# Attention and an S4 convolution on one core: two weight loads on another queue, and another order of the start

## The chip, the cores and the metric

One core of one Trainium2 chip. The metric is the device time of one launch in microseconds, the median of several runs. A core has TensorE (PE, matmuls), VectorE (DVE), ScalarE (ACT), GpSimd (POOL) and SyncE (SP, which here only issues DMAs), each with an instruction stream of its own; ACT and POOL issue DMAs too. The streams wait for each other on semaphores.

## The reference

```python
x = A_x                                   # 1 x 2048 x 448, bf16
g = sigmoid((x * gate_w).sum(-1))         # one gate per row
# a: attention, 16 heads of 28, one K and one V for all heads
q, k, v = x @ wq, x @ wk, x @ wv
a = softmax(q k^T / sqrt(28)) v, heads side by side, @ wo
# b: an S4 convolution of x along the rows, 448 channels, 256 modes
dt = exp(log_dt)
K[d, l] = Re sum_n C[d, n] * exp(dt * A[d, n] * l) * dt * B[d, n]
b = causal convolution of x with K, + x * Dskip    # the reference goes by FFT
out = g * a + (1 - g) * b
```

`A_re, A_im, B_re, B_im, C_re, C_im` are 448 x 256, and the output is 2048 x 448 in bf16. (In the setup the convolution's input is a tensor `u`, but the result uses `x` for both halves.)

## The kernel before, in words

**The attention.** The 2048 rows are four quarters of 512, the 16 heads four groups of 4: 16 blocks of one quarter and one group, each 64 tiles of 128 keys x 512 queries, 1024 tiles in all. `main` takes them in sets of 3 and 2 tiles. For each set PE makes the scores in PSUM (`qk`: line 1323 with four heads' rows of the array side by side from `qT`, or line 1332 as full matmuls from `qM`, a copy of `qT` by DMA with zeros for the other heads), ACT makes the exponential into `expT` (line 1357, 410 of them), and PE multiplies by V into `psB` (line 1383). Behind each block come the evacuation of `psB` and the division (`norm`, with a detour of the denominators through DRAM by POOL's DMAs), `outp` (multiplication by wo) and `fold` (gate and sum into `O`). `norm_last` does the division without the detour for the last two blocks.

**The convolution.** DVE builds tables of powers for 32 channels at a time (`masters`, `tables`, lines 991 to 1075); PE makes from them the taps K (`kgen`), which DVE puts into `kstg` and POOL's queue stores to `KP_scratch` in DRAM. SP loads them back as Toeplitz tiles T (`tload`, line 1131; 224 DMAs of 512 KB), PE multiplies them with `U`, a layout of x (`conv`, line 1155, two convs of 16 channels to each table), and DVE adds the result into `O`.

**The start.** `loads` issues the inputs. SP's queue carries, in this order: x's quarters 0 and 3 (natural layout, into `tab`), B_A_re and B_A_im as DMA transposes, wq, x's quarters 1 and 2 (`DQ`) as DMA transposes, and the other four parameters as DMA transposes. ACT's queue carries log_dt, wk, wv and the gate's weights. `prep_x` transposes quarters 0 and 3 on PE (line 718), evicts them to `xT` on ACT (line 728) where the pair (quarter, tile) is in `XA`, else on DVE (line 730), multiplies by wk (line 736), takes the largest |K| (line 742), and evicts K to `kT` on DVE (line 746) where the quarter is in `KD`, else on ACT (line 750). `Wb`, from the largest |K|, gives each query its offset below zero through one more matmul (`qproj`, line 963). `prep_params` computes the start values of the tables on DVE and ACT; ACT changes its function table three times (lines 862, 896, 911). The V weights are copied by DVE at line 645, the gate's at line 647.

**The order of everything.** No engine's order is written by hand. `Prog` collects all operations with their dependences and an estimated cost, and `schedule` puts them in order as a list planner: again and again it takes, of all ready operations, the one that can start first, ties by priority `pr` (lower first) and then by the place in the program. DMAs have an issue cost (`ISSUE`), a landing time (`DMA_NS` and `extra`) and a share of the DMA engines. Two things are special:

- Until the goal, the first exponential, operations that are not DMAs are picked by the length of the path from them to the goal, to which `RANK` adds a number of nanoseconds for single operations. `RANK` comes from a search. After the goal it has no effect.
- `idle` puts filler matmuls (line 1398, they add zero to `psB`) behind a PE operation where the planned matmul work of the last `SPAN` = 3413 ns is under `LOW` x `SPAN`, if the planned time is within `FILL` and the variable `part` is below 15:

```python
if self.part < 15 and self.FILL[0] < r < self.FILL[1] and busy < self.LOW * span:
...
pg.parts[len(pg.ops) - 1] = v % 16 if t < HF - 64 else 15
```

`HF` is 960, and `v` counts groups of four tiles.

Of the kernel before, what the change touches and what calls it, by code (L numbers as in the profile page):

```python
# [15 lines left out]
D = 448  # L16
H = 16
DH = 28
# [17 lines left out]
TW = 4 * 1024  # L36
XQ = NT * 512
SIN2PI = 6.2831850
XA = ((0, 1), (0, 2), (0, 3), (1, 0), (2, 2), (2, 3), (3, 0), (3, 1), (3, 2), (3, 3))
KD = (0, 1, 3)  # L40
GX = 3
DQ = (1, 2)
VNS = 140
# [32 lines left out]
def dram(t, off, dims):  # L76
    return bass.AP(tensor=t.tensor, offset=t.offset + off, ap=[list(d) for d in dims])
# [7 lines left out]
class Prog:  # L85
    SEM_NS = 56
    DMA_NS = 2200
    ISSUE = {"pool": 540.0, "sp": 470.0, "act": 470.0}
    LAT = {"pe": 170.0, "act": 173.0, "dve": 82.0, "pool": 85.0, "sp": 60.0}
    SAME = {"act": 100.0, "dve": 125.0, "pool": 150.0}  # L90
    SWITCH = 105.0
    BLOCK, FIRST, FETCH, IDLE, NEED = 256, 192, 5900.0, 3300.0, .015
    HALF = (21000.0, 21000.0, 1.8)
    HEAD = 0.6
    RANK = {111: 3000, 62: 3000, 39: -6000, 20: -3000, 30: -6000, 190: -6000, 46: -6000, 29: 700, 65: -6000, 84: 6000, 195: 6000, 40: -6000, 38: 3000, 33: 6000}
    POOL = (7,)
    LOW, SPAN, FILL = .53, 3413.0, (36000.0, 440000.0)
    AHEAD = 1500.0
    SLACK = {"pe": 700.0, "dve": 150.0}

    def __init__(self, nc, es):
        self.nc, self.es = nc, es
# [45 lines left out]
    def dma(self, pairs, desc, slot, rd=(), wr=(), pr=0, eng="sp", slow=False, extra=0, flip=False, cost=None, early=False):  # L148
        kw = dict(allow_slow_non_contiguous=True) if slow else {}

        def fn(e):
            if flip:
                return [e.dma_start_transpose(o, i) for o, i in pairs]
            return [e.dma_start(o, i, **kw) for o, i in pairs]  # L154
        nd, size = desc
        ns = 10.0 if size < 64 else 13.0 + 0.033 * size if size < 1500 else 8.0 + 0.0372 * size
        if cost is None:
            cost = nd * ns / 16.0 * (1.15 if size < 1500 else 1.0 if nd >= 512 else 1.4 if size < 3000 else 1.25)
        o = self.op(eng, fn, cost, rd, wr, pr)
        o.slot, o.ndma, o.extra = slot, len(pairs), extra + 200 * (early or flip)  # L160
        o.iss = len(pairs) * (1400.0 if flip else 640.0 if early else self.ISSUE[eng])
        prev = self.slots.get(slot)
        if prev is not None:
            o.deps[prev] = 1
        self.slots[slot] = o.i
        return o
# [268 lines left out]
def el(n, rate=0.96, fix=68):  # L435
    return fix + n / rate
# [22 lines left out]
class Kernel:  # L459
# [131 lines left out]
    def loads(self):  # L591
        pg, ins = self.pg, self.ins
# [33 lines left out]
        lx(QO[1])  # L626
        lraw(1)
        lraw(0)
        pg.dma(rows(wst, 0, ins["A_wq"], D), (448, 896), "wq", wr=["wqs"], cost=1500)
        lx(QO[2])  # L630
        lx(QO[3])
        pg.dma(rows(wks, 4 * DH, ins["A_wv"], DH), (448, 56), "wv", wr=["wvs"], eng="act", cost=150)
        pg.dma([(wks.v(0, P, 8 * DH, [[2, 3]]), dram(ins["gate_w"], 0, [[1, P], [P, 3]])),
                (wks.v(0, 64, 8 * DH + 6, [[1, 1]]), dram(ins["gate_w"], 384, [[1, 64], [1, 1]]))], (448, 2), "wg", wr=["wgs"], slow=True, eng="act", cost=150)
        for q in DQ:
            lx(q, True)
        pg.op("pool", lambda e: e.tensor_copy(self.Wk.v(0, P, 0, [[32, 16], [1, DH]]),
# [25 lines left out]
        for q in range(4):  # L663
            for j in (0, 2):
                u = 15 - 4 * q - j
                if q in DQ:
# [4 lines left out]
                    rd=[("xst", q)], wr=[("uf", q, j)], pr=0.6)  # L671
# [406 lines left out]
    def kgen(self, c):  # L1078
# [33 lines left out]
        for q in range(2):  # L1112
            lst = [(dram(self.KP, (32 * c + 16 * q + 4 * g) * KW, [[64, 32], [KW, 4], [1, 64]]),
                    ko.v(32 * g, 32, 256 * q, [[64, 4], [1, 64]])) for g in range(4)]
            pg.dma(lst, (512, 128), f"kw{q}", rd=["kst", "ksk"], wr=[("KP", c, q)], pr=0, eng="pool", extra=1800)

    def tbufs(self):
        n = NC * 8
# [19 lines left out]
    def conv(self, c):  # L1138
# [50 lines left out]
        pg.op("dve", lambda e: e.tensor_tensor(ov, ov, px.v(0, P, 0, [[1, 16], [16, 16]]), ALU.add),  # L1189
              el(256), rd=[Y], comm=tuple(("O" if c < 26 else "Oz", q) for q in range(7)), pr=2, unlock=px)  # L1190

    def outp(self, qc, tt):
        pg = self.pg
# [10 lines left out]
    def fold(self, qc, tt, px, off, n, rd, unlock=None):  # L1204
        tl = 4 * qc + tt
        ov = self.O.v(0, P, D * tl + off, [[1, n]])
        self.pg.op("dve", lambda e: e.scalar_tensor_tensor(ov, px(), self.gt.v(0, P, tl, [[1, 1]]), ov, ALU.mult, ALU.add),
                   el(n), rd=rd + ["gt"], comm=(("O", qc + tt * (qc == 3)), ("Oz", qc + tt * (qc == 3))), pr=2, unlock=unlock)

    def norm(self, i):  # L1210
        pg = self.pg
# [20 lines left out]
    def norm_last(self, i, o, n, bank, key):  # L1232
# [54 lines left out]
    def main(self):  # L1287
# [25 lines left out]
        def qk(s):  # L1313
# [165 lines left out]
```

## Time and profile before

| | |
|---|---|
| median of 3 runs | 506.75 us (506.19 to 508.49) |
| the profiled execution | 507.17 us, span 505.3 us, mean granted clock 0.985 |
| ACT busy | 482.6 us (96%), 466.2 of it in the 410 exponentials of line 1357 |
| DVE busy | 455.0 us (90%) |
| PE busy | 448.2 us (89%) |
| POOL busy | 165.3 us (33%) |
| first exponential | starts at 22.89 us |
| DMA | 139.51 MB, mean 276 GB/s |

Times in the profile are microseconds from the first instruction. A group's line gives busy time and mean duration (ns), then the engine's idle time before the group and what ended it. In a timeline a line gives start, duration, engine, source line, operation, output and inputs, and in brackets the idle time before it. In a table of windows each engine has its busy time and its number of instructions (x), then come the granted TensorE clock, the DMA engines' share and GB/s. "issue" is time in which an engine waited for nothing that the profile shows.

### The profile page before, as it was taken

How to read it: one execution, taken by the hardware profiler on the slowest of the kernel's cores; microseconds unless marked ns; L12 is line 12 of the kernel's file. 1: busy time of each engine (PE TensorE's matmuls, PEld its weight loads, DVE VectorE, ACT ScalarE, POOL GpSimd, SP SyncE). 2: the span in 40 equal slices, each digit the busy share in tenths (PEclk: the TensorE clock that was granted, in tenths of full speed). 3: DMA queues.
4: the chain of work that ended last, by engine and by line, in shares of the span. 5: the costliest groups of instructions: out<-in, count | busy, mean ns of one | idle time of the engine just before them, and what ended most of it. 6: DMA issues, size and time to landing. Idle time of an engine off the chain costs nothing.

```text
span 505.3 us, 18926 instructions
## 1 busy us (share of the span) xinstructions
PE 448.2 (89%) x8469; PEld 195.1 (39%) x8469; DVE 455.0 (90%) x834; ACT 482.6 (96%) x432; POOL 165.3 (33%) x308
## 2 busy tenths in 40 slices
PE   6797778898998999989898899999899999999885
PEld 2322213343433434334433344344343444344453
DVE  6899999999999999999999999999999999922334
ACT  5899999999999999999999999999999999999892
POOL 8533224252143520615332321435232152451000
PEclk8889999999999999999999999999999999999899
DMA  9977901979949797999989999599999979899982
GB/s 188 224 210 129 59 22 50 340 226 365 363 153 332 244 317 250 269 361 324 366 282 371 318 317 362 199 339 369 356 283 345 369 233 384 264 358 369 385 302 47
DMA packets 123395, 139.51 MB, mean 276 GB/s; under 512 B 56169, under 2 KB 63370, under 8 KB 123314
## 3 DMA queue, kind: packets, MB, share of 16 engines
q1 hardware_dynamic: 112208, 128.89, 79.8%
q0 software_dynamic: 8656, 9.25, 6.7%
q8 instruction: 66, 1.08, 0.9%
q10 hardware_dynamic: 2450, 0.17, 0.4%
q14 instruction: 15, 0.12, 0.1%
HBM read 125.18 MB, written 5.22 MB: 258 GB/s over the span
## 4 chain that ended last, share of the span: by engine, by line
ACT 48%; DVE 38%; PE 10%; issue 2%; DMA 1%; SPq 1%
ACT expT L1357 48%; DVE tab L1048 5%; DVE tab L1059 3%; DVE tab L1060 3%; DVE msq L991 3%; DVE tab L1070 2%; DVE tab L1058 2%; DVE tab L1057 2%; DVE mbf L1011 2%; PE psS L1332 2%; PE psB L1383 2%; DVE seedz L995 2%; PE psS L1323 2%; DVE seedz L993 1%; DVE tmp L1066 1%
## 5 line engine op out<-in xcount | busy, mean ns | idle before, releaser
L1357 ACT ACTIVATE expT<-psS 128x1536 bf16<-128x1536 f32 (+1 forms) x410 | 466.2, 1332 | 5.8 <-PE psS L1323 2.7
L1332 PE MATMUL psS<-qM,kT 128*128 128x512 bf16 (+2 forms) x455 | 122.5, 360 | 13.8 <-ACT expT L1357 10.5
L1383 PE MATMUL psB<-expT,vaug 128*32 128x512 bf16 (+2 forms) x1152 | 103.4, 366 | 3.1 <-issue 2.0
L1323 PE MATMUL psS<-qT,kT 29*128 29x512 bf16 (+2 forms) x699 | 82.1, 362 | 22.9 <-ACT expT L1357 21.5
L154 POOL DMA_DIRECT2D KP_scratch<-kstg x112 | 61.1, 553 | 65.6 <-DVE kstg L1110 37.4
L1048 DVE TENSOR_TENSOR tab<-tab,mbf 128x512 bf16<-128x512 bf16 (+3 forms) x56 | 64.6, 1154 | 0.0
L1383 PEld LDWEIGHTS psB<-expT,vaug 128*32 128x32 bf16 x1152 | 27.6, 93 | 76.1 <-issue 71.2
L154 POOL DMA_DIRECT2D rdenB<-R_scratch x56 | 28.4, 513 | 62.6 <-DMA R_scratch<-denT 53.7
L1332 PEld LDWEIGHTS psS<-qM,kT 128*128 128x128 bf16 x455 | 28.4, 97 | 50.7 <-ACT expT L1357 33.3
L1323 PEld LDWEIGHTS psS<-qT,kT 29*128 29x128 bf16 x699 | 21.4, 91 | 67.4 <-ACT expT L1357 53.6
L154 POOL DMA_DIRECT2D qM<-qT x64 | 32.2, 511 | 37.8 <-DVE qT L966 22.1
L1059 DVE TENSOR_TENSOR tab<-tab 128x1024 bf16<-128x1024 bf16 (+4 forms) x70 | 41.6, 595 | 0.0
L1060 DVE TENSOR_TENSOR tab<-tab 128x128 bf16<-128x128 bf16 (+4 forms) x70 | 41.5, 594 | 0.0
L1155 PE MATMUL psS<-T,U 128*32 128x128 bf16 (+3 forms) x1504 | 35.3, 220 | 0.3 <-DVE qT L966 0.3
L154 POOL DMA_DIRECT2D denT<-acc x14 | 10.0, 715 | 74.8 <-DVE kstg L1106 37.1
L1070 DVE TENSOR_TENSOR tab<-tab,tmp 128x4096 bf16<-128x4096 bf16 x14 | 32.0, 2285 | 0.1
L1058 DVE TENSOR_TENSOR tab<-tab,mbf 128x4096 bf16<-128x4096 bf16 x14 | 31.9, 2279 | 0.0
L1057 DVE TENSOR_TENSOR tab<-tab,mbf 128x4096 bf16<-128x4096 bf16 x14 | 31.9, 2276 | 0.0
L1155 PEld LDWEIGHTS psS<-T,U 128*32 128x32 bf16 (+3 forms) x1504 | 24.9, 94 | 13.8 <-issue 9.4
L1155 PE MATMUL psX<-T,U 128*32 128x128 bf16 (+7 forms) x1216 | 28.8, 222 | 0.1
L991 DVE TENSOR_TENSOR msq<-seedz 128x384 f32<-128x384 f32 (+1 forms) x50 | 27.1, 542 | 0.2
L1066 DVE TENSOR_TENSOR tmp<-tmp,mq 128x64 bf16<-128x64 bf16 (+4 forms) x70 | 25.3, 362 | 0.1
(160 smaller groups left out, 544.2 us busy)
## 6 DMA issues: line engine op xcount, KB each, us to landing
T<-KP_scratch SPq DMA_DIRECT2D x170, 512.0 KB, 9.1
U<-KP_scratch SPq DMA_DIRECT2D x40, 512.0 KB, 9.6
tab<-KP_scratch SPq DMA_DIRECT2D x14, 512.0 KB, 10.9
rdenB<-R_scratch POOLq DMA_DIRECT2D x56, 64.0 KB, 5.5
qM<-qT POOLq DMA_DIRECT2D x64, 32.0 KB, 5.1
tab<-in_A_x_dram SPq DMA_DIRECT2D x8, 224.0 KB, 3.6
O<-cst SPq DMA_DIRECT2D x1, 1792.0 KB, 9.9
KP_scratch<-kstg POOLq DMA_DIRECT2D x112, 16.0 KB, 4.1
```

Of the source, the lines that this page charges most:

```text
L154: return [e.dma_start(o, i, **kw) for o, i in pairs]
L991: pg.op("dve", lambda e: e.tensor_tensor(m2(msq), z2, z2, ALU.mult), el(2 * n), rd=[kr, ki] + first, wr=["msq"], pr=pr)
L1048: vo(lambda e, dst=dst, src=src, mri=mri: e.tensor_tensor(dst, src, mri, ALU.mult), 4 * n, done + mk(lv), [kr, ki, tk])
L1057: vo(lambda e, src=src, mi=mi, tv=tv: e.tensor_tensor(tv, src, mi, ALU.mult), 2 * n, done + mk(lv), [tk])
L1059: vo(lambda e, dc=dc, tc=tc: e.tensor_tensor(dc[0], dc[0], tc[1], ALU.subtract), n, [tk, kr], [kr])
L1060: vo(lambda e, dc=dc, tc=tc: e.tensor_tensor(dc[1], dc[1], tc[0], ALU.add), n, [tk, ki], [ki])
L1070: vo(lambda e: e.tensor_tensor(tab.v(0, P, FM, [[4, 1024], [1, 4]]), tab.v(0, P, lo + 124, [[CG, 32], [-4, 32], [1, 4]]), rho.v(0, P, 0, [ ...
L1155: r = e.matmul(ps.v(32 * j, 32 - 2 * n, 128 * k, [[1, 128]]), self.U.v(0, P, (4 * gi + j) * 32 + 2 * n, [[1, 32 - 2 * n]]), tbuf.v(0, P, t ...
L1323: r = e.matmul(self.psS.v(0, P, 512 * b + o, [[1, n]]), kT.v(32 * h, DH + 1, 128 * kt, [[1, 128]]), qT.v(32 * h, DH + 1, 512 * (i % 2) + q ...
L1332: r = e.matmul(self.psS.v(0, P, 512 * b + o, [[1, n]]), kT.v(0, P, 128 * kt, [[1, 128]]), self.qM.v(0, P, (i % 2) * XQ + 512 * h + qo, [[1 ...
L1357: pg.op("act", lambda e: e.activation(expT.v(0, P, 512 * es[0], spread(es, n)), self.psS.v(0, P, 512 * bs[0], spread(bs, n)), AF.Exp, scal ...
L1383: r = e.matmul(self.psB.v(32 * h, 32, qo, [[1, n]]), vaug.v(0, P, 32 * kt, [[1, 32]]), expT.v(0, P, 512 * ring[t] + o, [[1, n]]), start=(k ...
```

## The change: two loads, and the numbers of the planner

- The loads of wv and of the gate's weights (two DMAs each) are issued by POOL in place of ACT, with an expected landing 2500 ns later.
- The planner's numbers: an ACT issue costs 700 ns (470 before); DMA transposes and early x loads land 300 ns later than booked before, wq 300 later, the tap stores 600 earlier; `SLACK` of PE is 400 (700).
- Another `RANK` of 24 entries in place of 14, found by a search whose goal gives the first taps' landing more weight.
- `XA` and `KD`: x's tile (0, 2) is evicted by DVE, and K of quarter 3 by ACT. (The other entries of `XA` that change belong to quarters that PE does not transpose.)
- Fillers: `LOW` .49 (.53), `FILL` to 490 us (440).
- Priorities: `norm_last` that takes a free PSUM group has 0.9 in place of 1.5 (PE) and 2 (DVE); the folds of the last quarter and the last two convs' sums have 0.5 in place of 2.
- Sets 10 and up of three tiles take the row-tiled scores; before, from 12 on (set 10 alone is affected).

```diff
-XA = ((0, 1), (0, 2), (0, 3), (1, 0), (2, 2), (2, 3), (3, 0), (3, 1), (3, 2), (3, 3))
-KD = (0, 1, 3)
+XA = ((0, 1), (0, 3), (1, 2), (1, 3), (2, 0), (2, 1), (2, 3), (3, 0), (3, 1), (3, 2), (3, 3))
+KD = (0, 1)
...
-    ISSUE = {"pool": 540.0, "sp": 470.0, "act": 470.0}
+    ISSUE = {"pool": 540.0, "sp": 470.0, "act": 700.0}
...
-    RANK = {111: 3000, 62: 3000, 39: -6000, 20: -3000, 30: -6000, ...}
+    RANK = {39: -6000, 190: -3000, 81: 6000, 121: -6000, 193: -6000, ...}
-    LOW, SPAN, FILL = .53, 3413.0, (36000.0, 440000.0)
+    LOW, SPAN, FILL = .49, 3413.0, (36000.0, 490000.0)
-    SLACK = {"pe": 700.0, "dve": 150.0}
+    SLACK = {"pe": 400.0, "dve": 150.0}
...
-        o.slot, o.ndma, o.extra = slot, len(pairs), extra + 200 * (early or flip)
+        o.slot, o.ndma, o.extra = slot, len(pairs), extra + 500 * (early or flip)
...
-        pg.dma(rows(wst, 0, ins["A_wq"], D), (448, 896), "wq", wr=["wqs"], cost=1500)
+        pg.dma(rows(wst, 0, ins["A_wq"], D), (448, 896), "wq", wr=["wqs"], cost=1500, extra=300)
-        pg.dma(rows(wks, 4 * DH, ins["A_wv"], DH), (448, 56), "wv", wr=["wvs"], eng="act", cost=150)
+        pg.dma(rows(wks, 4 * DH, ins["A_wv"], DH), (448, 56), "wv", wr=["wvs"], eng="pool", cost=150, extra=2500)
...
-                (wks.v(0, 64, 8 * DH + 6, [[1, 1]]), dram(ins["gate_w"], 384, [[1, 64], [1, 1]]))], (448, 2), "wg", wr=["wgs"], slow=True, eng="act", cost=150)
+                (wks.v(0, 64, 8 * DH + 6, [[1, 1]]), dram(ins["gate_w"], 384, [[1, 64], [1, 1]]))], (448, 2), "wg", wr=["wgs"], slow=True, eng="pool", cost=150, extra=2500)
...
-            pg.dma(lst, (512, 128), f"kw{q}", rd=["kst", "ksk"], wr=[("KP", c, q)], pr=0, eng="pool", extra=1800)
+            pg.dma(lst, (512, 128), f"kw{q}", rd=["kst", "ksk"], wr=[("KP", c, q)], pr=0, eng="pool", extra=1200)
...
-            G, pe, dve = self.grp(), 1.5, 2
+            G, pe, dve = self.grp(), 0.9, 0.9
...
-            if s < 10 or 12 <= s < 411 and len(ts) == 3:
+            if s < 10 or 9 <= s < 411 and len(ts) == 3:
```

More of the change, by code (lines that the diff above doesn't have):

```diff
@@ L94 @@
     HEAD = 0.6
-    RANK = {111: 3000, 62: 3000, 39: -6000, 20: -3000, 30: -6000, 190: -6000, 46: -6000, 29: 700, 65: -6000, 84: 6000, 195: 6000, 40: -6000, 38: 3000, 33: 6000}
+    RANK = {39: -6000, 190: -3000, 81: 6000, 121: -6000, 193: -6000, 153: 3000, 160: -3000, 44: 700, 65: -6000, 43: -1500, 105: 3000, 198: -6000, 150: -6000, 84: 700, 29: -700, 25: -1500, 46: -1500, 47: -3000, 41: -3000, 199: -700, 137: -6000, 102: -1500, 20: 3000, 125: -6000}
     POOL = (7,)
-    LOW, SPAN, FILL = .53, 3413.0, (36000.0, 440000.0)
+    LOW, SPAN, FILL = .49, 3413.0, (36000.0, 490000.0)
     AHEAD = 1500.0
-    SLACK = {"pe": 700.0, "dve": 150.0}
+    SLACK = {"pe": 400.0, "dve": 150.0}
     def __init__(self, nc, es):
@@ L1189, in conv @@
         pg.op("dve", lambda e: e.tensor_tensor(ov, ov, px.v(0, P, 0, [[1, 16], [16, 16]]), ALU.add),
-              el(256), rd=[Y], comm=tuple(("O" if c < 26 else "Oz", q) for q in range(7)), pr=2, unlock=px)
+              el(256), rd=[Y], comm=tuple(("O" if c < 26 else "Oz", q) for q in range(7)), pr=(2, 0.5)[c > 25], unlock=px)
     def outp(self, qc, tt):
@@ L1207, in fold @@
         self.pg.op("dve", lambda e: e.scalar_tensor_tensor(ov, px(), self.gt.v(0, P, tl, [[1, 1]]), ov, ALU.mult, ALU.add),
-                   el(n), rd=rd + ["gt"], comm=(("O", qc + tt * (qc == 3)), ("Oz", qc + tt * (qc == 3))), pr=2, unlock=unlock)
+                   el(n), rd=rd + ["gt"], comm=(("O", qc + tt * (qc == 3)), ("Oz", qc + tt * (qc == 3))), pr=(2, 0.5)[qc == 3], unlock=unlock)
     def norm(self, i):
```

## The prediction

> **What bounds the kernel now.** I read the page's busy table and its groups first, then ScalarE's timeline, then the clock in windows of 2 to 5 us, then the waits of SyncE's queue. The page:
>
> ```profile
> span 505.3 us, 18926 instructions
> ...
> PE 448.2 (89%) x8469; PEld 195.1 (39%) x8469; DVE 455.0 (90%) x834; ACT 482.6 (96%) x432; POOL 165.3 (33%) x308
> ...
> L1357 ACT ACTIVATE expT<-psS 128x1536 bf16<-128x1536 f32 (+1 forms) x410 | 466.2, 1332 | 5.8 <-PE psS L1323 2.7
> ```
>
> ACT is the bound, by one group: 410 softmax exponentials that take 466.2 us together and stand idle for only 5.8 us between them. The first starts at 22.89 us, and the last ends at 494.7 + 0.7 = 495.4. So the span is 22.9 of prelude, 472.5 of exponentials (466.2 + 5.8, and 0.9 of two small activations that fall between them) and 9.9 of tail. The change can only win in the prelude, the 5.8 and the tail. The prelude on ACT:
>
> ```profile
> 2.44 1.31 ACTq L154 DMA_DIRECT2D seedw<-in_A_wv_dram  x2
> 3.77 1.30 ACTq L154 DMA_DIRECT2D seedw<-in_gate_w_dram  x2
> 5.10 1.28 ACT L862 ACT_TABLE_LOAD   x1 [5.10 <-issue]
> ...
> 7.45 1.66 ACT L728 ACTIVATE xT<-psS 128x512 bf16<-128x512 f32 x3
> 9.18 0.60 ACT L728 ACTIVATE O<-psS 128x512 bf16<-128x512 f32 x1
> 10.06 0.95 ACT L891 ACTIVATE T<-T 128x896 f32<-128x896 f32 x1 [0.29 <-DVE T L888]
> ...
> 13.44 1.06 ACT L728 ACTIVATE O<-psS 128x512 bf16<-128x512 f32 x2
> 15.92 0.60 ACT L728 ACTIVATE O<-psS 128x512 bf16<-128x512 f32 x1 [1.42 <-PE psS L718]
> ...
> 21.59 1.28 ACT L911 ACT_TABLE_LOAD   x1
> 22.89 1.45 ACT L1357 ACTIVATE expT<-psS 128x1536 bf16<-128x1536 f32 x1
> ```
>
> ACT issues the four DMAs of the change from 2.44 to 5.07, then works from 5.10 to 22.87 with 0.29 + 1.42 = 1.7 idle: the first exponential starts as its last table load ends. The other chain into it ends beside it (QK matmuls at 22.02 to 22.62). Two side views matter below, the clock and the first tap loads:
>
> ```profile
> 10.00:12.00 2.00, 1.86 (x8) 0.68 (x6) 1.93 (x3) 1.94 (x3) 1.82 (x4) 0.50 1.19 190
> ...
> 26.00:28.00 2.00, 2.00 (x12) 0.48 (x10) 2.00 (x4) 2.00 (x2) 2.00 (x1) 0.58 0.95 341
> ...
> 475.00:480.00 5.00, 4.50 (x100) 2.79 (x103) 0.00 (x0) 3.37 (x4) 0.00 (x0) 0.69 1.05 386
> ...
> SPq L1131 <- DMA KP_scratch<-kstg: 71.8, 7, 41.1
> ```
>
> The number behind the five busy times is the granted clock: halved in the prelude, around 26 to 30, and around 477 to 480. The last line says that SyncE stood 41.1 us (until 85.0) for the first convolution taps.
>
> **Step 1, V's and the gate's weights to GpSimd's queue.** Four issues leave ACT: 1.31 + 1.30 = 2.6 us. ACT's table load then starts at 2.4 and ends at 3.7; its first activation waits for the dt matmul, which ends at 3.46 + 0.55 = 4.0. So ACT's work starts 6.39 - 4.05 = 2.3 earlier (if the table load waits for that matmul too, 1.0 earlier). On POOL the cost is four issues. The cheap row is a 128-packet store of taps, 553 ns; the dear one is denT's load of 128 runs of 64 B, 715 ns. Two of the four have 384 runs; if time went with runs they would cost 3 x 0.55 = 1.7 each. So POOL pays 4 x 0.55 = 2.2 to 2 x 1.7 + 2 x 0.55 = 4.5; I take 2.4, as issues of 128 and 32 runs (553 and 511) hardly differ. Behind them on POOL stand the identity (its select ends at 1.58; the first transposes need it at 4.97), the K weights' copy (5.25 to 5.81; first used at 9.42), four copies into U and the memsets of qM (done at 16.8; qM's first DMA issues at 22.3). Slack is 3.4, 3.6 and 5.5 us, so 2.4 is hidden; at 4.5 the K copy would be late by about 0.9, which is beside work that waits for x anyway until 14. Cost 0, bounds 0 to +0.9.
>
> V's copy on DVE (L645) waited 1.31 us for this load, until 7.63, with the next DVE operand landing at 8.87. From POOL, last issue at about 2 to 3 and landing 2.7 to 5.5 after it (POOL's rows), the weights land at 5 to 8.5. Cost 0, bounds -0.1 to +0.4. [...]
>
> **Step 2, the prelude's other order.** The table of ranks acts only before the first exponential. XA's entries for quarters 1 and 2 do nothing (those are transposed by DMA); the live one moves the x eviction (0, 2) from ACT to DVE: ACT -0.59. KD moves quarter 3's K eviction to ACT: +0.68 (row L750), DVE -0.74 +0.69. How early can the first exponential be?
> - ACT: B_A_re lands at 8.87 as before (SyncE's queue keeps its order), so L891 stays at 10.06. Behind it stand 0.95, five moduli of 0.87, a table load 1.28, two sines 0.97 and a table load 1.28: 9.8, that is 19.9. Ahead of it, from 4.05, ACT needs 0.54 + 0.58 + 2 x 0.59 + 4 x 0.59 = 4.7 of 6.0 us: three of quarter 3's evictions, which stood at 13.4 and 15.9 behind the moduli, now fit (just so in the 4.7 us that a table load held back would leave), and I let the last spill 0.4. With the K eviction 0.68: 19.9 + 0.4 + 0.68 = 21.0.
> - The x chain: the last x transpose issues at 12.1 and lands 4.0 later, 16.1; four K matmuls 1.03, maximum 0.68, Wb 0.35, bias matmul 0.39, cast 0.68, QK 0.60: 19.8, and 21.2 with two other DVE operations of 0.7 in between.
>
> I take 21.2, a gain of 22.9 - 21.2 = 1.7; bounds 0 (the order wastes it) to 2.6 (ACT at 20.3, K eviction hidden).
>
> **Step 3, the loop.** Set 10 goes from three full matmuls to three row-tiled ones side by side: PE saves 0.4 us where ACT is not waiting; 0. Every later operation may be re-ordered, since the list planner starts from other times. I leave the 5.8 at 5.8, bounds -3.6 to +6. Fillers: the threshold falls from .53 to .49 of 3.4 us, 0.14 us of matmul per window, so some of 36 fillers go (12.7 us of PE, mostly at 40 to 100 us). FILL's longer end is void: fillers need part < 15, which is 15 from tile 896 on, about 436 us. The halved clock at 477 stays possible.
>
> **Step 4, the tail.** norm_last and the last folds go ahead of convolution work. The page's tail is the last convolution: its matmuls start at 496.96, then 0.69, 0.45 and 0.42 us of work and 4.4 us of output store. The one operation ahead of the final normalization is 0.36 us. Gain 0, bounds -0.5 to +1.
>
> **Sum.** The profiled execution took 507.17 with a span of 505.3, 0.4 above the median of 506.75. 507.2 - 1.7 = 505.5 for such an execution, 505.0 for the median. About 0.5% (2.5 us) is what a measurement of this kernel can tell from no change: under 504.2 is faster, over 509.3 slower.
>
> **Rivals.**
> - *The loop's stalls shrink as well (0.29).* Two of them, 0.81 and 0.83 us at 475 and 479 beside the halved clock, and 2 us of singles before; an order better fitted to DMA latencies could drop 1.8: 505.0 - 1.8 = 503.2. For: the store's and issue's costs move towards the rows (an ACT issue 650 ns, booked 470, now 700). Against: those gaps follow PE's "issue" pauses (1.29 us at 474), which no booked cost names.
> - *The clock drops more often (0.25), slower.* [...] Price: the drop at 26.3 to 29.7 left ACT idle 0.27 + 0.22 + 0.61 = 1.1, the one at 477 0.83. Five more windows cost 4.8: 509.8; from five on it is slower, below that it eats the gain. [...]
> - *The freed time is not used (0.09).* V's copy late at DVE's head, or the x chain keeps its place: 506.8.
>
> **Chances.** Forecast 0.37, of which 0.06 lies under 504.2. Faster 0.29 + 0.06 = 0.35; same 0.31 + 0.09 = 0.40; slower 0.25. The range 502.0 to 510.2 takes in 503.2 less a tail gain, and the clock's 509.8. The forecast's own is 503.5 to 506.5.
>
> **What would show it.** Right: no wv or gate issue on ACT's timeline, the first activation near 4.1, all L728 of quarter 3 before 11, the first exponential at 20.3 to 21.5; group L1357 at 466 with idle near 5.8; last exponential to end 9.9. Wrong: DVE L645 waiting past 8.9; the first exponential still near 22.9; a granted clock under 1.00 in windows between 40 and 470; L1357's idle at 8 or more; or the first tap load later than 85 with SyncE's queue still loading taps past 490.

## The result, and the profile after

The changed kernel takes 513.34 us (median of 6 runs, 510.63 to 514.22) against 507.18 for the kernel before on the same chip: a ratio of 1.0117 (95% interval 1.009 to 1.0143). Slower by 1.2% where 505.0 was forecast, and above the range's 510.2. The profiled execution took 513.72 us with a mean granted clock of 0.975. Its page, and the waits of SyncE's queue:

```profile
span 511.8 us, 18807 instructions
...
PE 432.0 (84%) x8357; PEld 195.0 (38%) x8463; DVE 457.3 (89%) x834; ACT 482.8 (94%) x432; POOL 166.3 (33%) x312
...
L1357 ACT ACTIVATE expT<-psS 128x1536 bf16<-128x1536 f32 (+1 forms) x410 | 466.5, 1339 | 12.5 <-PE psS L1323 5.8
```

```profile
SPq L1131 <- DMA KP_scratch<-kstg: 68.3, 7, 44.3
```

The exponentials take what they took (466.5 us, 466.2 before). What grew is ACT's idle time between them, from 5.8 to 12.5. Gaps of 0.13 us and more in ACT's timeline, by stage, and the difference of the two spans (6.5 us):

| us | before | after | difference |
|---|---|---|---|
| first exponential | 22.89 | 22.45 | -0.4 |
| ACT idle up to 60 us | 1.1 | 4.2 | +3.1 |
| 60 to 440 us | 2.4 | 3.0 | +0.6 |
| from 440 us | 2.0 | 4.7 | +2.8 |
| last exponential to end | 9.9 | 10.1 | +0.2 |

The start, in the timeline of all engines:

```profile
1.39 1.44 POOL L154 DMA_DIRECT2D seedw<-in_A_wv_dram  x2 [0.38 <-issue]
...
2.91 0.31 POOL L542 TENSOR_SCALAR_AFFINE_SELECT ident<-ident 128x128 bf16<-128x128 bf16 x1
3.15 1.33 POOL L154 DMA_DIRECT2D seedw<-in_gate_w_dram  x2
...
3.28 1.46 PE L554 MATMUL psS<-ident 128*128 128x512 bf16 x3 [3.28 <-POOL ident L542]
...
4.68 0.55 PE L854 MATMUL psX<-cst 1*128 1x448 bf16 x1
...
5.26 0.54 ACT L862 ACTIVATE cst<-psX 128x448 bf16<-128x448 f32 x1 [1.55 <-PE psX L854]
```

The bracket at the end of a line is the idle time in front of it. ACT's issues are gone and its table load starts at 2.43, but its first activation starts at 5.26 and not near 4.05, 1.55 us after the load: it waits for the dt matmul, which stands on PE behind the warm-ups (L554), which wait for the identity, and that stands on POOL behind V's weights.

The early loss in ACT's timeline (before, it had one unbroken row of 19 exponentials here, from 33.07 to 54.7):

```profile
37.97 3.46 ACT L1357 ACTIVATE expT<-psS 128x1024 bf16<-128x1024 f32 x3 [2.13 <-PE psS L1332]
41.67 2.36 ACT L1357 ACTIVATE expT<-psS 128x1536 bf16<-128x1536 f32 x2 [0.23 <-PE psS L1323]
44.87 4.63 ACT L1357 ACTIVATE expT<-psS 128x1536 bf16<-128x1536 f32 x4 [0.84 <-PE psS L830]
```

PE's and DVE's timelines say what PE was late for, and POOL's what lay beside DVE:

```profile
35.62 0.61 PE L963 MATMUL psX<-qT,Wb 128*128 128x512 bf16 x1 [1.59 <-DVE qT L960]
40.90 0.39 PE L820 MATMUL psS<-onT,gt 128*16 128x128 f32 x2 [1.01 <-DVE gt L801]
43.50 0.88 PE L830 MATMUL psS<-acc,onT 16*128 16x64 f32 x6 [1.01 <-DVE acc L824]
```

```profile
24.29 2.00 DVE L888 TENSOR_TENSOR mbf<-T,cst 128x896 f32<-128x896 bf16 x1
...
34.87 0.69 DVE L960 TENSOR_REDUCE qT<-psX 128x512 bf16<-128x512 f32 x1
...
39.26 1.58 DVE L801 TENSOR_SCALAR gt<-gt 128x16 f32<-128x16 f32 x1
40.77 0.28 DVE L1011 CAST mbf<-seedz 128x256 bf16<-128x256 f32 x1
40.97 1.25 DVE L991 TENSOR_TENSOR msq<-seedz 128x256 f32<-128x256 f32 x1
42.25 1.00 DVE L993 SCALAR_TENSOR_TENSOR seedz<-seedz 128x128 f32<-128x128 f32 x1
43.17 0.27 DVE L824 COPY acc<-psS 16x128 f32<-16x128 f32 x1
...
43.88 0.42 DVE L991 TENSOR_TENSOR msq<-seedz 128x256 f32<-128x256 f32 x1
```

```profile
24.30 1.04 POOL L668 COPY U<-tab 128x896 bf16<-128x896 bf16 x1
...
39.77 3.33 POOL L668 COPY U<-tab 128x896 bf16<-128x896 bf16 x3
```

While POOL's three copies into U run (39.77 to 43.10), three of DVE's small instructions take 1.0 to 1.6 us; the same L991 takes 0.42 once they are over. (L801 starts 0.51 us ahead of the first of these copies; what held it until then no view shows.) All three lie ahead of what PE waits for in its order (L801 for L820; L991 and L993 for L824, and that for L830). The largest gap, 2.13 us in front of 37.97, lies ahead of them: PE stood 1.59 us at L963 for L960, and ahead of L960 in DVE's row stands L888 at 24.29, which took 2.00 us beside the copy at 24.30 (1.08 before the change). The matmuls behind L963 then ran at a clock of 0.50 (36 to 38 us). The same place before the change:

```profile
39.91 0.19 DVE L801 TENSOR_SCALAR gt<-gt 128x16 f32<-128x16 f32 x1
...
40.68 1.59 DVE L1011 CAST mbf<-seedz 128x256 bf16<-128x256 f32 x1
42.19 1.29 DVE L991 TENSOR_TENSOR msq<-seedz 128x256 f32<-128x256 f32 x1
...
44.05 0.27 DVE L824 COPY acc<-psS 16x128 f32<-16x128 f32 x1
```

There two copies ran from 41.07 on, after L801. They held L1011 and L991 as much, and L824 came even later (44.05, 43.17 after), but PE's order had L830 later too (44.37, 43.50 after), so PE hardly waited. What counts is where PE's order puts the instruction that waits. DVE had no slack in either kernel. The window from 22 to 52 us, before and after (the busy times are those of PE, PEld, DVE, ACT and POOL):

```profile
22.00:52.00 30.00, 25.25 (x217) 8.68 (x216) 29.28 (x71) 28.83 (x27) 11.95 (x12) 0.94 0.80 177
```

```profile
22.00:52.00 30.00, 24.61 (x163) 7.44 (x165) 29.11 (x67) 25.50 (x25) 8.26 (x12) 0.84 0.79 177
```

DVE was busy 29.28 us of 30 before and 29.11 after. An instruction that is held beside a copy counts as busy here: of the 29.11, some 3.9 us are the excess of the four slowed instructions above (0.9, 1.4, 0.8 and 0.7).

### The profile page after: what moved, and what is told of

It is laid out like the page before. It is cut to its first block, busy times and chain, and to the rows that moved or that the text cites. A ratio compares the mean times of both kernels' runs of the same rounds, so it can differ in the third digit from the quotient of the medians.

```text
span 511.8 us, 18807 instructions
## 1 busy us (share of the span) xinstructions
PE 432.0 (84%) x8357; PEld 195.0 (38%) x8463; DVE 457.3 (89%) x834; ACT 482.8 (94%) x432; POOL 166.3 (33%) x312
## 3 DMA queue, kind: packets, MB, share of 16 engines
q8 instruction: 66, 1.08, 0.9%
## 4 chain that ended last, share of the span: by engine, by line
DVE 45%; ACT 31%; PE 20%; issue 2%; DMA 1%; SPq 1%
ACT expT L1357 31%; DVE tab L1048 7%; DVE tab L1059 4%; DVE tab L1058 4%; DVE tab L1057 4%; PE psS L1332 4%; DVE tab L1060 4%; PE psB L1383 3%; PE psS L1323 3%; DVE tab L1070 3%; DVE tmp L1066 2%; DVE msq L991 2%; PE psS L1155 2%; PE psX L1155 1%; DVE T L888 1%
## 5 line engine op out<-in xcount | busy, mean ns | idle before, releaser
L1357 ACT ACTIVATE expT<-psS 128x1536 bf16<-128x1536 f32 (+1 forms) x410 | 466.5, 1339 | 12.5 <-PE psS L1323 5.8
L1332 PE MATMUL psS<-qM,kT 128*128 128x512 bf16 (+2 forms) x360 | 103.5, 363 | 27.0 <-ACT expT L1357 12.7
L1323 PE MATMUL psS<-qT,kT 29*128 29x512 bf16 (+2 forms) x702 | 84.7, 368 | 27.4 <-ACT expT L1357 24.8
L1383 PE MATMUL psB<-expT,vaug 128*32 128x512 bf16 (+2 forms) x1152 | 105.1, 370 | 2.6 <-issue 1.9
L1323 PEld LDWEIGHTS psS<-qT,kT 29*128 29x128 bf16 x702 | 22.1, 92 | 74.0 <-ACT expT L1357 57.3
L1332 PEld LDWEIGHTS psS<-qM,kT 128*128 128x128 bf16 x452 | 29.7, 100 | 46.1 <-ACT expT L1357 29.2
L1155 PE MATMUL psX<-T,U 128*32 128x128 bf16 (+7 forms) x1408 | 34.4, 222 | 0.7 <-issue 0.5
L1155 PE MATMUL psS<-T,U 128*32 128x128 bf16 (+7 forms) x1312 | 31.1, 221 | 0.8 <-DVE qT L966 0.4
L1155 PEld LDWEIGHTS psX<-T,U 128*32 128x32 bf16 (+7 forms) x1408 | 23.8, 95 | 13.9 <-issue 10.3
L1095 PE MATMUL psS<-tab 128*32 128x64 bf16 x1152 | 27.3, 242 | 1.1 <-DVE tab L1075 1.1
L991 DVE TENSOR_TENSOR msq<-seedz 128x384 f32<-128x384 f32 (+1 forms) x50 | 27.2, 544 | 0.1
L1155 PEld LDWEIGHTS psS<-T,U 128*32 128x32 bf16 (+7 forms) x1312 | 21.4, 93 | 14.8 <-issue 10.9
```

Of the source, the lines that this page charges most:

```text
L1155: r = e.matmul(ps.v(32 * j, 32 - 2 * n, 128 * k, [[1, 128]]), self.U.v(0, P, (4 * gi + j) * 32 + 2 * n, [[1, 32 - 2 * n]]), tbuf.v(0, P, t ...
L1323: r = e.matmul(self.psS.v(0, P, 512 * b + o, [[1, n]]), kT.v(32 * h, DH + 1, 128 * kt, [[1, 128]]), qT.v(32 * h, DH + 1, 512 * (i % 2) + q ...
L1332: r = e.matmul(self.psS.v(0, P, 512 * b + o, [[1, n]]), kT.v(0, P, 128 * kt, [[1, 128]]), self.qM.v(0, P, (i % 2) * XQ + 512 * h + qo, [[1 ...
L1357: pg.op("act", lambda e: e.activation(expT.v(0, P, 512 * es[0], spread(es, n)), self.psS.v(0, P, 512 * bs[0], spread(bs, n)), AF.Exp, scal ...
L1383: r = e.matmul(self.psB.v(32 * h, 32, qo, [[1, n]]), vaug.v(0, P, 32 * kt, [[1, 32]]), expT.v(0, P, 512 * ring[t] + o, [[1, n]]), start=(k ...
```

## The experiments

Theories. **D**: from 22 to 52 us DVE sets the pace, and PE, in its own order, waits for it; whatever DVE loses there comes out at ACT. **F**, a conjecture: PE pauses at one place of each block of 256 instructions of its stream (before's instruction queue moves 66 packets, and 16938 PE instructions in 66 packets are 257 each), and the planner's order is fitted to where these places fall. **L**: the time after 440 us is lost to convolution work left over. Rival **A**: the clock, lower through fewer fillers, costs the time.

**The planner's numbers one by one.** a_low53, the changed kernel with the filler numbers of before:

```diff
-    LOW, SPAN, FILL = .49, 3413.0, (36000.0, 490000.0)
+    LOW, SPAN, FILL = .53, 3413.0, (36000.0, 440000.0)
```

> The changed kernel with the filler settings of before (LOW .53, FILL to 440 us). In the profile of the changed kernel the granted clock is 0.5 at 35.5 to 38.9, 45.8 to 52.6, 469.0 to 472.4 and 482.7 to 489.5 us, and the exponentials idle 12.5 us in place of 5.8. Theory A (fewer fillers let the clock fall): more fillers than 30, the early drop at 45.8 goes, idle falls to about 9, time 509 to 511. Theory B (PE is held up by single badly placed waits; the clock falls as a consequence, and late PE work decides the rest): the hole at 34 to 36 us and the drop after it stay, the late drops stay, time 512.5 to 514. Theory C (the whole new order is worse at random): any other order, 508 to 514.

513.33 us, 1.0139 (1.0085 to 1.0193): nothing won. b_low49, the other way round, the kernel before with the new filler numbers:

> The kernel before with the filler settings of the changed one (LOW .49, FILL to 490 us). Theory A: the clock falls in one to three windows between 40 and 110 us, ACT idles 2 to 5 us more there, time 509 to 512. Theory B: no drop before 460, time 506 to 508. FILL's longer end adds no filler after 436 us in either.

510.04 us, 1.0056 (1.0027 to 1.0084), with 1.1 us of idle before 60 us as in before: the 0.5% comes from 200 to 440 us (5.8 idle, 2.4 before). The filler numbers had re-ordered DVE and PE there, and seven fillers fewer (29) also shift PE's later instructions (theory F); this run can't tell the two apart. a_prio, the changed kernel with the priorities of `norm_last`, the folds and the sums as before:

> The changed kernel with the priorities of before for norm_last, the last folds and the last two convs' sums. Order differs only on PE and DVE after about 455 us. The late part (from 462 us) idles ACT 4.6 us in the changed kernel and 1.8 in before. If the new priorities cause that (they pull norm_last's fp32 matmul and others ahead of conv work): late idle falls to about 2, time 510 to 511.5. If it is due to what is left of convolution work and the instruction supply there: late idle 4 to 5, time 512.5 to 514.

514.0 us, 1.0148 (1.0099 to 1.0197), and 6.3 us idle from 440 us on: they aren't the late loss. And a_lat, the changed kernel with a planned latency 2 us longer for block 1's L960, which sets L963 later on PE:

> The changed kernel, with the planner told that the largest-|Q| reduction of block 1 (line 960) becomes available 2 us later. On PE the bias matmul of that block (line 963) then moves behind set 11's four score matmuls and one group of V matmuls; in the changed kernel it stood ahead of them and held PE 1.9 us (33.9 to 35.6), and ACT then idled 2.13 us at 35.85 to 37.97. Theory B: ACT's idle of 2.1 us goes, and with it the halved clock from 35.5 on; with the rest of the order as it falls, 509 to 512. Theory A: the hole moves the time by its own 2 us at most, the drop at 45.8 to 52.6 stays, 511 to 512. Theory C: no relation, 508 to 514.

514.16 us, 1.0149 (1.0102 to 1.0196). The early idle fell to 3.0, and the re-planned rest took it back (5.4 from 200 to 440 us).

**The clock.** a_fill is the changed kernel with fillers that the planner doesn't count, in PE's planned pauses from 30 to 56 us; a_late has the full score matmuls doubled from set 380 on; b_both is the kernel before with both:

```diff
+        self.fill.update({order[-1]: int((r - free) / 218.0)} if not k and self.part < 15 and 30000.0 < r < 56000.0 and r - free > 218.0 else {})
...
-                for o, kt, qo, n in parts * m:
+                for o, kt, qo, n in parts * (m if s < 380 or hasattr(e, "n") else 2 * m):
```

> The changed kernel, with fillers in every idle stretch of the plan between 30 and 56 us; the order of all other instructions on every engine stays that of the changed kernel. Theory A (the clock): the halved clock at 35.5 to 38.9 and 45.8 to 52.6 goes at least in part, ACT's idle before 60 us falls from 4.2 to 1.5 to 3, the rest stays, time 510.5 to 512.5. Theory B (PE stands in single waits): idle before 60 us stays at about 4, time 513 to 514.5.

522.26 us, 1.0302 (1.026 to 1.0345). With 13 more rows of fillers (21 matmuls) it took 9 us more. ACT's idle before 60 us did not fall (6.1), and from 60 to 440 us it was 10.3 where the changed kernel has 3.0, behind "issue" pauses of PE of 1 to 2.5 us.

> The changed kernel, in which from set 380 on (about 460 us) each full score matmul is issued twice (it writes the same scores again); nothing else moves on any engine. In the changed kernel the clock is halved at 469.0 to 472.4 and 482.7 to 489.5, and ACT idles 4.7 us after 440. Theory A: no halved clock there, late idle about 2 to 3, time 511 to 512. Theory B: the doubled matmuls only take PE time, late idle 4.5 to 6, time 513 to 515.

515.15 us, 1.0176 (1.0146 to 1.0206). The halved clock at the end was gone (full from 53.7 to 511 us), and the idle from 440 us on stayed at 4.5: the late loss isn't the clock's. Its early loss lay behind the three copies alone (1.5 and 1.7 us in front of 40.2 and 44.5), without the gap at L963: which wait loses isn't the same in every execution of this order.

> The kernel before with both additions: fillers in every planned idle stretch between 30 and 56 us and doubled full score matmuls from set 380 on; the order of the rest is the same. Its clock is halved in the loop at 26.3 to 29.7 and 476.9 to 480.3, with 0.83 us idle at the latter. Theory A: the late drop goes, time 505 to 506.5, better than both kernels. Theory B: 506.5 to 508.

523.58 us, 1.0335 (1.0286 to 1.0385), with before's own order.

**Where the blocks lie.** Tiny matmuls (4 columns) that no plan counts, early in PE's stream of before: in sh13 13 pairs (weight load and matmul, 26 instructions) behind the first warm-up, in sh128 128 pairs (256 instructions) ahead of the first L954. The line of sh13, then that of sh128:

```diff
+                    for _ in range(13 if e == "pe" and i == self.order[e][0] else 0):
+                        self.tiny(x)
...
+                    for _ in range(128 if i == self.mark else 0):
+                        self.tiny(x)
```

> The kernel before, with 13 tiny matmul pairs (4 columns; 26 PE instructions, a tenth of a 256-instruction block) behind PE's first warm-up, not counted by the planner; nothing else moves. Theory F (PE's code comes in blocks of 256 instructions, and a hole of about a microsecond follows each; the order is fitted to where the blocks end): the holes fall on other instructions, ACT's idle time from 60 us on rises from 4.4 us to 10 to 18, and the time to 513 to 525 us, although the added work is about 1 us in the prelude. Rival (where the blocks end doesn't matter; b_both and a_fill lost time by the work added): 506.5 to 508 us, idle from 60 us on within 2 us of before.

> The kernel before, with 128 tiny matmul pairs (4 columns, 256 PE instructions, one whole block) ahead of PE's first L954, not counted by the planner; nothing else moves. At the 40 ns that a pair took in sh13 they take 5.2 us from 11 us on, of which 2.2 lie in PE's wait for Wq, so the first exponential comes 2 to 3.5 us later (24 to 25.5 us). Theory F (PE's code comes in blocks of 256 instructions and the order is fitted to where they end): one whole block leaves the fit as it was, so ACT's idle time from 60 us on is 4 to 6.5 us (4.4 in before, 11.9 with a tenth of a block), and the time is 508 to 510.5 us, under sh13's 513.4 although ten times the work was added. Rival (the loss in sh13 came of the added work, or of any shift): idle from 60 us on 10 us or more, 514 to 525 us.

sh13 took 513.38 us, 1.0131 (1.0089 to 1.0173); sh128, with ten times the work and the first exponential 1.6 us later, 509.64, 1.0054 (1.0021 to 1.0087). The exponentials' line of sh13, then of sh128 (other line numbers, same operation), and the instruction queue, of before and of sh128:

```profile
L1361 ACT ACTIVATE expT<-psS 128x1536 bf16<-128x1536 f32 (+1 forms) x410 | 466.0, 1336 | 13.2 <-PE psS L1327 11.2
```

```profile
L1362 ACT ACTIVATE expT<-psS 128x1536 bf16<-128x1536 f32 (+1 forms) x410 | 465.8, 1332 | 6.7 <-PE psS L1328 3.2
```

```profile
q8 instruction: 66, 1.08, 0.9%
```

```profile
q8 instruction: 67, 1.10, 0.9%
```

26 instructions more, a tenth of F's block, brought 13.2 us of idle, 256 more 6.7 (5.8 without any). From 60 us on it is 11.9, 5.3 and 4.4. The queue moves 66 packets of 16 KB, and with 256 more instructions 67. The place of the pauses agrees: in the traces of before, after, sh13 and sh128 PE's weight loads have 38 pauses of 0.5 us and more marked "issue" from 25 us on, and 33 of them lie at places 136 to 182 of a block of 256, counted by weight loads at two instructions each; spread evenly, 7 would. So the place of PE's stream within 256 instructions is shown to matter; that PE pauses in each block is not (before's trace has 8 of these pauses, the changed kernel's 10). This bounds every other experiment: a shift of PE's stream by 26 instructions brought 7.5 us of idle by itself (sh13). a_fill and b_both shift it as well, so what they lost can't be split, and any re-planning draws anew.

**The late loss.** So the changed kernel's stream was shifted at 421 us only, by 28 instructions (a_sl13) and by 128 (a_sl64):

```diff
+                for o, kt, qo, n in (parts[:1] * 7 if s == self.lt and not hasattr(e, "n") else []):     # a_sl64: 32
+                    e.matmul(self.psS.v(0, P, 512 * b + o, [[1, 4]]), kT.v(0, P, 128 * kt, [[1, 128]]),
...
```

> The changed kernel with 14 tiny matmul pairs (28 PE instructions) ahead of two score matmuls of L1332 at about 421 us, not counted by the planner; nothing before them moves. Theory F for the late loss: the blocks end on other instructions from there on, and ACT's idle time after 440 us (4.7 us; 4.0 to 6.3 in the runs whose late code stood at the same place of the blocks) becomes another: under 3.3 or over 7. Rival (the late loss is DVE's and the folds' lateness, as theory L says): it stays at 4 to 6.5 us. Total 510.5 to 516.

> As a_sl13, with 64 tiny pairs (128 PE instructions, half a block; about 2.5 us of PE's time at 421 us). Theory F: idle after 440 us differs from a_sl13's by over 1.5 us and from the changed kernel's 4.7, to either side. Rival: 4 to 6.5 us again, with up to 1 us more at 421 us for the work itself. Total 510 to 517.

513.56 us (1.0127, 1.0095 to 1.0159) and 515.03 us (1.0165, 1.0127 to 1.0203). The idle from 440 us on was 4.6 and 3.7: other holes, no other sum in the first, and less by 1.1 in the second, which lost 4 us at 418 to 425 itself. Of the pauses counted above, the changed kernel's trace has only one behind 440 us (at 481.5). So F wasn't shown to be the late loss either; it stays open.

**The weights alone.** b_pool is the kernel before with only the two loads on POOL's queue (the loop's order on every engine as before):

```diff
-        pg.dma(rows(wks, 4 * DH, ins["A_wv"], DH), (448, 56), "wv", wr=["wvs"], eng="act", cost=150)
+        pg.dma(rows(wks, 4 * DH, ins["A_wv"], DH), (448, 56), "wv", wr=["wvs"], eng="pool", cost=150, extra=2500)
...
```

> The kernel before, with V's and the gate's weights loaded by POOL's queue and nothing else; RANK and all numbers as before, and from the first block on the order is the same on every engine. This is the headline part of the change alone. Prediction's step 1: the first exponential at 21 to 22 (22.89 before), time 505.5 to 506.5. If the identity behind the weights' issues on POOL holds the dt matmul (in the changed kernel that matmul started 1.2 us later, and ACT's first activation at 5.26, not at 4.05): first exponential 22.3 to 22.9, time 506 to 507.5.

507.94 us, 1.0034 (1.0016 to 1.0051), so no gain at all. Its page:

```profile
L1357 ACT ACTIVATE expT<-psS 128x1536 bf16<-128x1536 f32 (+1 forms) x410 | 465.7, 1339 | 6.7 <-PE psS L830 2.2
```

The first exponential came at 22.01, 0.9 earlier than in before's profile (but no earlier than the 21.6 to 21.9 of three other profiles of before's start, see below), and 2.25 us went at once in one gap at 43.7, where PE waited 1.5 us at L830 for DVE's L824 (43.59, only 0.46 earlier than before). b_low49, whose first exponential came at 21.90, had L824 at 42.99 and no such gap. (The gate's load is edited in the same way.) To see whether it is that wait alone, L830 was set five groups later on PE (b_pool_mv), and in the changed kernel L963, L820 and L830 three, three and seven groups later (a_mv):

```diff
+            pe.insert(k + n, pe.pop(k))        # b_pool_mv: L830 by 5; a_mv: L963 by 3, L820 by 3, L830 by 7
```

> The kernel before with the two weights on POOL's queue, and the gate's matmul L830 set five PE instruction groups later in PE's own order (behind two groups of three L1323 and one of two L1332); every other queue is as in b_pool. Theory D (DVE paces 20 to 46 us, and PE waits in order at L830 behind DVE's L824): ACT's idle stretch of 2.25 us at 43.7 goes to under 0.7, idle before 60 us falls from 2.82 to about 1.2, first exponential near 22.0; 505.0 to 506.3 us, 0.1 to 1.5 below the kernel before, if the same score matmuls as there are hit by fetches later. Rival (the early gain is lost wherever, since DVE's work as a whole is late): the wait moves to the next matmul that needs DVE, idle before 60 us stays at 2.3 to 3, 507 to 508 us.

> The changed kernel with three matmuls set later in PE's order: block 1's L963 by three groups, the gate's L820 by three and L830 by seven; the other queues are as in the changed kernel. Theory D: ACT's idle time before 60 us falls from 4.2 us to 1 to 2, and with PE busier in 35 to 50 us the halved clock there goes or shrinks; the late part (4.7 us of idle after 440 us) stays, so 510 to 512 us against the changed kernel's 513.3. Rival (the clock, not the in-order waits, costs the early time; moving the matmuls does nothing): idle before 60 us stays over 3.5 us, 513 to 514 us.

b_pool_mv: 509.12 us, 1.0037 (1.0012 to 1.0061). The gap at 43.7 went, and 2.4 us of idle came in its place at 47 to 60 us: the rival's result, and a median above its time. (The profile is of the fastest of the 12 runs, 505.86 us, so it doesn't show where the median lost its time.) a_mv: 513.31 us, 1.0124 (1.0093 to 1.0155): early idle 2.2 (4.2), 1.9 more from 60 to 200 us, and no time won. Moving the waits on PE only moves the loss, as long as DVE is as late as it is.

**The start.** a_mvid is a_mv with the identity ahead of V's weights on POOL, and a_sp the changed kernel with wq's load behind x's transposing loads on SP; both by the same edit of the finished order:

> a_mv, and on POOL's queue the identity's L542 set ahead of V's weights' two issues (V's weights issue 0.3 us later). It tests the step of the prediction that failed in the prelude. Theory: ident is ready at 1.6 us instead of 3.2, the warm-ups start at 1.6 instead of 3.28, the step's matmul L854 ends near 4.0 and ACT's first activation starts at 4.0 to 4.2 us instead of 5.26 and ACT's idle stretch ahead of it goes. First exponential: by the prediction's own step 2 down by up to 1.1 us (22.45 to 21.4); by theory D by 0 to 0.5, since the x chain behind it waits for PE's L736 and DVE. Total 509.5 to 512 us; no more than 1 us from a_mv.

515.09 us, 1.0153 (1.0117 to 1.0189). ACT's first activation came at 3.74 (5.27), and the first exponential at 23.25, no earlier than the other runs of that start.

> The changed kernel with one step moved on SP's queue: wq's two loads are issued behind the four transposing loads of x and not ahead of the first two; every other queue is the same. Theory (the first exponential hangs on SP's row of transposing loads, which the move of V's and the gate's weights never touched): PE's first L736 on T, which waits for that load at 13.6 us (13.2 to 14.4 in the runs), starts 1.0 to 1.3 us earlier, at 12.1 to 12.6, and the first exponential comes at 21.0 to 22.0 us (22.45; 22.7 on average over the runs of that order). By theory D the gain is given back before 60 us: the time is 512 to 513.5 us. Rival (DVE's chain to Wb sets the first exponential): it stays at 22.3 to 23.2 us whatever L736 does.

514.37 us, 1.014 (1.0112 to 1.0169). The load's part held:

```profile
12.34 1.04 PE L751 MATMUL psS<-T,expT 128*128 128x512 bf16 x4 [1.73 <-DMA T<-in_A_x_dram]
16.11 0.35 DVE L654 COPY Wq<-mbf 128x448 bf16<-128x448 bf16 x1 [1.09 <-DMA mbf<-in_A_wq_dram]
```

K's first matmul on T (L736 elsewhere) started at 12.34 instead of 13.58, but wq now landed last, and the first exponential stood at 22.91. Several chains end within a microsecond of each other there; no single one of them is worth much.

**What slows DVE.** POOL's copies of quarters 1 and 2 into U, held until DVE has copied omq (L835), all else in its place, in the changed kernel (a_ul) and in b_pool (b_pool_ul):

```diff
+        self.ops[us[0]].deps[x] = 1        # us: the last four copies on POOL, behind the second qM store; x: DVE's L835
```

> The changed kernel with the same edit (copies into U at 24.3 and three from 39.8 us held until DVE's L835, 45.2 us). Theory D: L801 at 39.3 us takes 0.2 instead of 1.58, L991 and L993 at 41 to 42 us 0.4 and 0.3 instead of 1.25 and 1.00; DVE's L801 comes 1 us and its L824 3 us earlier, PE's waits at L820 and L830 shrink; idle before 60 us falls from 3 to 4.8 us (the runs of that order) to 1.2 to 2.5, the rest stays: 511 to 512.7 us against 513.3. Rival: idle before 60 us stays over 3 us, or the time stays at 513 to 514.5 since the clock then halves elsewhere.

> b_pool (the kernel before with the two weights on POOL's queue) with the last four of POOL's copies into U (L668; two at 23.3 and two at 40.6 us in b_pool) held until DVE has copied omq (L835, 45.9 us); every queue's own order is otherwise as it was. Theory D with its source (DVE is 97% busy from 22 to 52 us, and single DVE instructions beside a POOL copy take 1.3 to 2.0 us instead of 0.3 to 1.1): L1011 and L991 at 40 to 43 us take 0.3 and 0.4 again, DVE's L824 comes 2 to 3.5 us earlier (40.5 to 41.8; 43.6 in b_pool), ACT's idle stretch of 2.25 us at 43.7 goes, and idle before 60 us falls from 2.82 to 0.8 to 1.6; some of it is given back at 55 us, since the copies then lie beside DVE's work of 46 to 50 us. 505.5 to 507.3 us (507.9 in b_pool). Rival (DVE's own work is too long whatever lies beside it; or PE's clock): the idle stretch stays or moves, idle before 60 us over 2.2 us, 507.5 to 509 us.

a_ul: 508.95 us (median of 11, 507.07 to 511.23), 1.0043 (1.0021 to 1.0064). That is 2.4 us above the kernel before on its chip, where the changed kernel was 6.2 above: 3.8 us are gone, more than the 0.6 to 2.3 that D had expected. DVE's timeline, ACT's, and the window of 40 to 47 us (lines are 17 or 18 higher: 906 is 888, 978 is 960, 818 is 801, 841 is 824, 853 is 835):

```profile
23.57 1.08 DVE L906 TENSOR_TENSOR mbf<-T,cst 128x896 f32<-128x896 bf16 x1
...
33.23 0.69 DVE L978 TENSOR_REDUCE qT<-psX 128x512 bf16<-128x512 f32 x1
...
37.62 0.17 DVE L818 TENSOR_SCALAR gt<-gt 128x16 f32<-128x16 f32 x1
...
38.61 0.27 DVE L841 COPY acc<-psS 16x128 f32<-16x128 f32 x1
...
40.64 0.28 DVE L853 COPY omq<-psS 128x128 f32<-128x128 f32 x1
```

```profile
33.08 12.90 ACT L1375 ACTIVATE expT<-psS 128x1024 bf16<-128x1024 f32 x11
46.31 8.32 ACT L1375 ACTIVATE expT<-psS 128x1536 bf16<-128x1536 f32 x7 [0.33 <-PE psS L1341]
```

```profile
40.00:47.00 7.00, 6.64 (x35) 1.52 (x35) 6.69 (x13) 6.52 (x7) 4.53 (x4) 0.52 0.46 110
```

L801 takes 0.17 again and L824 comes 4.6 us earlier (38.61, 43.17). Of these, 2.9 us are the three copies' and 0.9 the copy's at 24.3 (L888 takes 1.08 again); the other 0.7 DVE had already at 23.57, by a start that no edit touched. PE's wait at L963 is 0.24 us (1.59), and ACT's idle before 60 us is 0.33 us, better than before the change. The copies slow DVE no less where they are now (L993 and L995 took 1.0 at 41 to 45 us), but nothing that PE waits for stands behind them. And the last table: PE's clock was halved in nearly the whole window (0.52), and ACT lost 0.33 us. In b_pool_ul, 508.38 us, 1.0024 (1.0002 to 1.0046), the gap at 43.7 went too, but 1.1 us at 57 (PE's L963 waiting for DVE's L960, with the copies now beside DVE at 46 to 50) and more at 59 to 63 took its place, with the first exponential at 23.1 in the profiled run: idle up to 60 us 2.3, and 0.9 more in the gap that ends at 60.5, so there the rival's number came. No version beat the kernel before.

## Why the prediction was wrong, point by point

**Step 1, the cost on POOL: right in size, wrong in what stood behind it.** The four issues took 1.44 + 1.33 = 2.8 us (2.4 forecast, 2.2 to 4.5 bounds). V's weights landed 3.2 to 3.4 us after their issue, with DVE's memsets (the last ends at 6.3) beside them, and DVE's L645 ran unhindered at 7.86. What failed is "the first transposes need it at 4.97": PE takes the warm-ups and the dt matmul first, in order, and those wait for the identity. ACT's start gained 1.1 us and not 2.3. a_mvid gave the rest back, and nothing came of it.

**Step 2, a gain of 1.7: mis-sized, and from a base that was one draw.** The start of before, also that of b_low49, b_both and (with its 13 tiny pairs) sh13, gave 22.89, 21.90, 21.64 and 21.93 for the first exponential, 22.1 on average, with 22.89 the latest: the clock was halved from 9.3 to 16.1 us in that one. The changed start gave 21.89 to 23.99 over ten profiles, 22.7 on average. By these averages the gain is -0.6, by the two profiles of the result 0.4, and not 1.7. The x chain of the prediction (16.1 for the last x transpose, then 5.1) left out that PE's first matmul on the transposed x waits for its load until 13.2 to 14.4 us, with 2.1 to 3.3 us of idle time before it, after which PE ran on a halved clock in seven of the ten. Those seven had the first exponential at 22.45 to 23.99, the other three at 21.89 to 22.15.

**Step 3, "I leave the 5.8 at 5.8": the step that decided it.** The prediction says that every later operation may be re-ordered and puts that at nothing without a reason. The bound was taken from the whole span (ACT, 5.8 us idle), but the stretch from 22 to 52 us has another: DVE, busy 29.28 of 30 us before the change. The busy row of the page (DVE 90%) hides that, the row of that window shows it. There the re-planned order set POOL's copies beside L888, L801, L991 and L993, and PE's in-order waits passed the delay on (3.1 us more idle up to 60 us); a_ul takes that early part back. The 2.8 us from 440 us on are the same step's, and their cause stays open. The upper bound of +6 wasn't a price of anything, and the measured +6.7 lies past it. Of the 8.3 us between forecast and result 6.7 are this term, 1.3 the gain of step 2 that didn't come (0.4 and not 1.7, by the two profiles), and 0.2 the tail.

**The rival of the clock: the right side, by the wrong mechanism.** The clock did drop more often, as it said (35.5 to 38.9, 45.7 to 52.6, 469.0 to 472.4, 482.7 to 489.5), and in the changed kernel's six runs a lower mean clock goes with a longer time (2.8 us for 0.01; a_lat's four runs show no such slope). But ahead of 35.5 and 45.7 PE had stood idle first, waiting for DVE (1.59 and 1.01 us). In a_ul the clock was halved for 7 us at 0.33 us of idle; in a_late it was full and the late loss stayed. So the price of 1.1 us a window was read from windows whose clock was only part of what they lost. The five more windows of the 509.8 stand in no run: the changed kernel's trace has 20.5 us of halved clock in the loop, before's 6.8, so four more of 3.4 us. How busy PE has to be for a full clock, no run shows: in the 3.4 us ahead of the two drops in before's loop PE was busy 2.56 and 1.82 us.

**Fillers and the other two rivals.** 30 fillers against 36, as forecast; their number is not what costs (a_low53). The stalls didn't shrink, and "freed time not used" holds for the weights alone (b_pool).

**Step 4** held: 10.08 us against 9.87. **What the prediction named as showing it wrong** did: idle of 12.5 in L1357's group, a granted clock below 1.00 in 45 to 53 us, the first tap load at 88.1 us (85.0), though SP's tap loads ended at 482.3 (478.4) and not past 490.

**Open:** the 2.4 us that a_ul still lacks. Its idle from 60 us on was 8.1 (4.4 before): 4.6 from 60 to 440 us (2.4) and 3.5 from 440 on (2.0). The late idle is 3.5 to 6.3 us in all runs with the changed order but a_fill's 2.4, and 1.6 to 2.6 in those with before's start of the blocks (b_low49 among them, with seven fillers fewer). The priorities, the filler numbers and the clock were ruled out; the leftover convolution work was larger in the changed order (448 weight loads of L1155 behind the 380th exponential, 408 before), but no run took that away alone.

## What to carry to other kernels

Look for the bound stage by stage: a window of 30 us in which another engine is 97% busy decides what a start 1 us earlier is worth, whatever bounds the other 470. Where two engines slow each other (here DVE's L801 from 0.19 to 1.58 us, POOL's two copies to 5.85), ask which of the slowed instructions somebody waits for in order, and put the disturbing work behind it; that was worth 3.8 us here, and moving the waiting instruction itself was worth none. Before a gain of 1 us is booked, see how far the same code varies from run to run: here the first exponential by 1.3 to 2.1 us.

## What the runs showed of the hardware

- **Where PE's pauses fall.** In before the instruction queue moved 66 packets of 16 KB, one every 7.7 us on average (66 in 505 us), for 16938 PE instructions, 257 a packet. Of PE's 38 pauses of 0.5 us and more, shown as "issue", in four traces, 33 lie in the same fifth of a block of 256. A shift of 26 instructions cost 6.4 us; one of 256 cost 2.8, with the start 1.6 later in its profile.
- **DVE beside a POOL copy.** In the changed kernel L801, 128x16 in f32, took 1.58 us instead of 0.19, and L991 1.25 instead of 0.42: 0.8 to 1.4 us more, where one copy took 1.0 to 1.1 us. It fell out the other way in the kernel before: the two copies from 24.41 on took 5.85 us, and the two L888 at 24.91 and 26.45 their usual 1.08. Why the one or the other, no view shows. What held L801 in the 0.51 us ahead of the copy stays open.
- **A halved clock that cost little.** In a_ul from 40 to 47 us, at a clock of 0.52 and with PE busy 6.64 of 7.00 us, ACT stood idle for 0.33 us; a row of 11 exponentials ran unbroken into it, up to 45.98.
